# Attention and a maxout layer on one core: weight differences moved up in VectorE's order, half of the copies of transposed w2 on ScalarE, h of the second block ahead of x of the second group

## The chip, the core and the metric

The kernel runs on one core of a Trainium2 chip. A core has TensorE (matmuls; PE in the profile, with its weight loads as PEld), VectorE (DVE), ScalarE (ACT), GpSimd (POOL) and SyncE (SP, which here only issues transfers). Each engine works through its own instructions in program order, and the engines wait for each other with semaphores. The metric is the device time of one launch in microseconds, the median of several runs.

## The reference

Block-causal attention over 8 batches, 8 heads, 576 positions and head size 64 (blocks of 64 positions; a position sees its own block and all earlier ones), and then a maxout layer over the 4608 tokens:

```python
def _attn_ref(q, k, v) -> np.ndarray:
    ...
    scores = scale * np.matmul(q, k.transpose(0, 1, 3, 2))
    ...
    attn = attn / (np.sum(attn, axis=-1, keepdims=True) + 1e-09)
    return np.matmul(attn, v).astype(np.float32)

def _moe_ref(x, w1, w2, w_out) -> np.ndarray:
    h1 = x @ w1
    h2 = x @ w2
    g = np.maximum(h1, h2)
    return (g @ w_out).astype(np.float32)
```

x has 512 columns, w1 and w2 are 512 x 1024, w_out is 1024 x 512. Inputs and the output are fp32.

## The kernel before

**An identity saves a matmul.** max(x w1, x w2) = x w2 + max(x (w1 - w2), 0). So the kernel computes d = w1 - w2 once (`diff_w`, into `d_sb`), g = max(x d, 0) (`h_unit`), the product M = w2 w_out once (`m_unit`, into `m_sb`), and y = x M + g w_out (`y_unit`). For M it needs w2 transposed; `bT_unit` does that on TensorE and copies the result from PSUM into `bT_sb`. There are four weight column blocks j of 256 columns: each has one difference (1024 elements per partition), and one `bT_unit` of eight 128 x 128 transposes and one copy (line 229). h unit f covers 128 columns of d, so h units 2j and 2j+1 read difference j.

**Attention.** Two heads make a pair (32 pairs), two pairs a group (16 groups g). `load_qk` brings q and k of a group, GpSimd casts them to bf16 (`cast`, line 132), TensorE transposes them (`transposes`, line 352), and two engines copy the result from PSUM (line 360). Scores are matmuls into one of two PSUM buffers (`ps_s`), ScalarE takes the exponential (line 395), GpSimd clears the masked corners. `av` multiplies by v (line 479); VectorE takes the reciprocal of the sums (line 485) and multiplies (line 486) into `xp`. `x_out` transposes xp of a group on TensorE (lines 517 and 519) and copies it into `xT` (lines 522 and 523), the x of the maxout layer. All other PSUM results share one pool of four buffers (`ps_m`, tag "m"), handed out in turn.

**Order.** The order is written out by hand: each call below appends to the queues of the engines that it uses. The maxout units stand in a list, `todo`, in a fixed order: for the first 256 tokens h 0, h 1, bT 0, h 2, h 3, bT 1 and so on, then h of the next 320 tokens, then the M units, then y. Each has a number of matmuls, a cost for each (256 columns cost 0.5, 320 cost 0.625, a transpose of w2 0.25) and the number of tokens of x that it needs. `fill(n)` emits units from the list until a cost of n is used up; it takes the first whose tokens are done (`done_tokens`). `fill_of(g)` spreads the ready work over the groups to come.

**The stretch that the change touches** is lines 641 to 682, batch 0's last attention work and the start of batch 1. GpSimd's part of it: five loads of v of batch 1 (lines 651 and 652), and `load_qk(3, ..., gated=True)` at line 653. "Gated" means that GpSimd first writes one column of the destination (line 119), so that the transfer, issued by SyncE, can't start before GpSimd gets there. Later (lines 671 to 680) GpSimd casts q and k of group 3, and TensorE transposes them in the middle of a `fill` of n:

```python
    cast("q", 3, ((pool, 0, RPP),))
    cast("k", 3, ((pool, 0, RPP),))
    n = fill_of(GPB)
    fill(n // 2)
    transposes("q", 3, (dve, act))()
```

By the code's counts n is 32 here: 16 before the transposes of q, about 26 matmuls of 320 columns.

Of the kernel before, what the change touches and what calls it, by code (L numbers as in the profile page):

```python
# [14 lines left out]
def kernel(  # L15
# [10 lines left out]
    nc = tc.nc  # L26
# [83 lines left out]
    dve, pool, act = nc.vector.tensor_copy, nc.gpsimd.tensor_copy, nc.scalar.copy  # L110

    def load_qk(g, queues, gated=False):
        b, u = divmod(g, GPB)
        for nm, src, queue in (("q", q, queues[0]), ("k", k, queues[1])):
            if queue is None:
                continue
            raws[nm, g] = t = raw.tile([P, 2, RPP * D], FP32, name=f"{nm}raw")
            if gated:
                nc.gpsimd.memset(t[:, 0, :1], 0.0)
            queue.dma_start(  # L120
                out=t[:],
                in_=src[b, 4 * u:4 * u + 4].rearrange(
                    "(s h) (p t) d -> (h p) s (t d)", h=2, t=RPP),
            )

    def cast(nm, g, parts):
        t = raws[nm, g].rearrange("p s (t d) -> p t s d", d=D)
        if (nm, g) not in qk_n:
            qk_n[nm, g] = qkn.tile([P, RPP, 2, D], BF16, name=f"{nm}n")
        n = qk_n[nm, g]  # L130
        for copy, j0, j1 in parts:
            copy(out=n[:, j0:j1], in_=t[:, j0:j1])  # L132
# [27 lines left out]
    def diff_w(j):  # L160
        fs = slice(j * WB, (j + 1) * WB)
        nc.vector.tensor_sub(d_sb[:, :, fs], w1_raw[j][:], w2_sb[j])  # L162
# [8 lines left out]
    dve, pool, act = nc.vector.tensor_copy, nc.gpsimd.tensor_copy, nc.scalar.copy  # L171
# [51 lines left out]
    def bT_unit(j):  # L223
        pt = ps_m.tile([P, 2, NDM, P], BF16, name="ps_bT", tag="m")
        for i in range(2):
            for c in range(NDM):
                nc.tensor.transpose(pt[:, i, c, :], w2_sb[j][:, c, i * P:(i + 1) * P], ident[:])
                if i == 1 and c == NDM - 1:
                    nc.vector.tensor_copy(
                        out=bT_sb[:, 2 * j:2 * j + 2, :],  # L230
                        in_=pt.rearrange("p i c d -> p i (c d)"))
                yield
# [52 lines left out]
    def plan():  # L285
        def h(i, f):
            t0, w = spans[i]
            units.append((h_unit(i, f), t0 + w, w / SPAN, NDM))

        def y(i, s, last=False):  # L290
            t0, w = spans[i]
            if last:
                units.append((y_last(i, s), t0 + w, 0.333, 3 * NY))
            else:
                units.append((y_unit(i, s), t0 + w, 1.0, NY))

        for i in range(NSPAN):
            for f in range(NFF):
                h(i, f)
                if i == 0 and f % 2:  # L300
                    units.append((bT_unit(f // 2), 0, 0.25, 2 * NDM))
                if i > 2 and f % 2 == 0 and f // 2 < tiles[i - 1]:
                    y(i - 1, f // 2)
            if i == 1:
                for n in range(2 * NDM):
                    units.append((m_unit(n // NDM, n % NDM), 0, 0.5, NFF))
                for j in range(2):
                    for s in range(tiles[j]):
                        y(j, s)
        n = tiles[-1]  # L310
        for s in range(n):
            y(NSPAN - 1, s, s == n - 1)
# [9 lines left out]
    def fill(n):  # L322
        while n > 0:
            if not current:
                k = next((k for k, t in enumerate(todo) if t[2] <= done_tokens[0]), None)
                if k is None:
                    return max(0, n)
                current.append(todo.pop(k))
            t = current[0]
            next(t[1])  # L330
            n -= t[3]
            t[0] -= 1
            if not t[0]:
                current.pop()
        return 0
# [96 lines left out]
    def tile_0(p):  # L432
        u = ps_s.tile([P, 2, 512], FP32, name="ps_s", tag="s")
        scores(p, u, 0, 0, 0, 512)
        return lambda: (exp(p, u, 512, 0), mask(p, 0))

    def tile_1(p):
        u = ps_s.tile([P, 2, 512], FP32, name="ps_s", tag="s")
        scores(p, u, 0, 0, 512, 64)
        scores(p, u, 64, 1, 128, 448)  # L440
        return lambda: (exp(p, u, 512, 512), mask(p, 576))

    def tile_2(p):
        u = ps_s.tile([P, 2, 512], FP32, name="ps_s", tag="s")
        corner_scores(p, u, 320)
        scores(p, u, 0, 2, 256, 320)
        scores(p, u, 384, 3, 448, P)

        def out():
            exp(p, u, 512, 1024)  # L450
            nc.scalar.activation(
                out=aT_r[p % NA][BLK:, :, 1536:AW], in_=u[BLK:, :, 320:320 + BLK],
                func=AF.Exp, scale=scale,
            )
            mask(p, 1024)
            mask(p, 1344)
        return out

    def region(*tiles):
        for out in tiles:  # L460
            out()

    def av(p, ts):
        b, hp = divmod(p, HP)
        vv = vv_r[b % NV]
        a = aT_r[p % NA]
        n = len(ts)
        h0 = hp // 2 * 4 + hp % 2
        if p % 2 == 0 and ts[0] == 0:
            xps[p // 2] = xpool.tile([P, 2, NCH, 2, D], BF16, name="xp")  # L470
        xp = xps[p // 2]
        po = ps_m.tile([P, n, 2, D + 1], FP32, name="ps_o", tag="m")
        n_mm = 2 * sum(t + 1 for t in ts)
        mm = 0
        for gi, t in enumerate(ts):
            for hh in range(2):
                for c in range(t + 1):
                    a0 = a_col(p, c, t)
                    nc.tensor.matmul(  # L479
                        po[:, gi, hh, :], a[:, hh, a0:a0 + P], vv[:, c, h0 + 2 * hh, :],  # L480
                        start=(mm == 0), stop=(mm == n_mm - 1),
                    )
                    mm += 1
        rec = small.tile([P, 3, 2, 1], FP32, name="rec")
        nc.vector.reciprocal(rec[:, :n, :, 0], po[:, :, :, D])  # L485
        nc.vector.tensor_mul(  # L486
            xp[:, :, ts[0]:ts[0] + n, p % 2].rearrange("q s t d -> q t s d"), po[:, :, :, :D],
            rec[:, :n].to_broadcast([P, n, 2, D]),
        )

    def x_by_dma(g):
        return BY_DMA <= g < NG - 1
# [10 lines left out]
    def x_out(g, t0=0, t1=NCH, copies=(dve, dve)):  # L503
        b, u = divmod(g, GPB)
        if x_by_dma(g):
            if u == GPB - 1:
                done_tokens[0] = (b + 1) * S
            return
        xp = xps[g]
        n = t1 - t0  # L510
        n_odd = min(t1, NCH - 1) - t0
        pe = ps_m.tile([P, 2, n, BLK], BF16, name="ps_xe", tag="m")
        po = ps_m.tile([P, 2, n_odd, BLK], BF16, name="ps_xo", tag="m")
        for s in range(2):
            for t in range(t0, t1):
                src = xp[:, s, t].rearrange("p a d -> p (a d)")
                nc.tensor.transpose(pe[:, s, t - t0, :], src[:BLK], ident[:BLK, :BLK])
                if t < NCH - 1:
                    nc.tensor.transpose(po[:, s, t - t0, :], src[BLK:], ident[BLK:, BLK:])
        dst = xT[:, 2 * u:2 * u + 2, b * S + t0 * P:b * S + t1 * P].rearrange(  # L520
            "p s (t h w) -> p s t h w", h=2, w=BLK)
        copies[0](out=dst[:, :, :, 0], in_=pe[:])
        copies[1](out=dst[:, :, :n_odd, 1], in_=po[:])
        if u == GPB - 1:
            done_tokens[0] = min(b * S + t1 * P, (b + 1) * S)
# [126 lines left out]
        load_v(1, c)  # L652
    load_qk(3, (SP, SP), gated=True)
    x_out(0, 2, NCH)
    fill(2)
    diff_w(1)
    outs = tile_0(4), tile_1(4)
    av(3, [2, 3, 4])
    region(*outs)
    x_out(1, 2, NCH)  # L660
    fill(4)
    diff_w(2)
    fill(2)
    region(tile_2(4), tile_0(5))
    fill(4)
    diff_w(3)
    fill(2)
    region(tile_1(5), tile_2(5))
    fill(4)
    fill(2)  # L670
    cast("q", 3, ((pool, 0, RPP),))
    cast("k", 3, ((pool, 0, RPP),))
    n = fill_of(GPB)
# [86 lines left out]
```

The softmax here doesn't subtract the row's maximum and nothing guards it: scores larger than these inputs give would overflow.

## Time and profile before

| what | before |
|---|---|
| device time, median of 3 runs | 260.99 us (260.82 to 261.92) |
| span of the profiled execution | 259.2 us |
| PE busy | 244.8 us, 94% |
| DVE busy | 137.6 us, 53% |
| ACT busy | 141.3 us, 55% |
| POOL busy | 109.8 us, 42% |
| granted TensorE clock | 1.0 |
| PE's share of the chain that ended last | 85% |
| one weight difference on DVE (line 162) | 1.22 us, four of them |
| one copy of transposed w2 on DVE (line 229) | 0.69 us, four of them |

A busy share is an average over the whole span; TensorE at 94% still has stretches in which it stands. The profile cuts the span into 40 slices of 6.48 us and gives the busy share of each engine in tenths, which shows where those stretches are. For each of them the trace then tells which instruction waited, for which engine and line, and for how long. The chain that ended last is followed back from the last instruction, at each step to what released it; a stretch of the span in which the chain lies on another engine, or on a transfer, isn't set by TensorE.

### The profile page before, as it was taken

How to read it: one execution, taken by the hardware profiler on the slowest of the kernel's cores; microseconds unless marked ns; L12 is line 12 of the kernel's file. 1: busy time of each engine (PE TensorE's matmuls, PEld its weight loads, DVE VectorE, ACT ScalarE, POOL GpSimd, SP SyncE). 2: the span in 40 equal slices, each digit the busy share in tenths (PEclk: the TensorE clock that was granted, in tenths of full speed). 3: DMA queues.
4: the chain of work that ended last, by engine and by line, in shares of the span. 5: the costliest groups of instructions: out<-in, count | busy, mean ns of one | idle time of the engine just before them, and what ended most of it. 6: DMA issues, size and time to landing. Idle time of an engine off the chain costs nothing.

```text
span 259.2 us, 7161 instructions
## 1 busy us (share of the span) xinstructions
PE 244.8 (94%) x2949; PEld 139.4 (54%) x2983; DVE 137.6 (53%) x301; ACT 141.3 (55%) x198; POOL 109.8 (42%) x274
## 2 busy tenths in 40 slices
PE   8688799999999999999999999999999999999995
PEld 3346566856555545454646464646464655444444
DVE  4967996646584518451855185518550853453200
ACT  2798552766665766576657665776577431100111
POOL 2987914475638163816381638263823010000000
DMA  7999998789579995998599949984986122202122
GB/s 245 317 204 310 194 241 146 280 73 275 111 184 250 135 195 136 238 149 215 129 236 139 179 163 239 141 208 139 90 106 116 44 51 83 83 0 81 43 104 99
DMA packets 71265, 41.30 MB, mean 159 GB/s; under 512 B 53568, under 2 KB 58048, under 8 KB 71232
## 3 DMA queue, kind: packets, MB, share of 16 engines
q1 hardware_dynamic: 28544, 31.27, 41.4%
q0 software_dynamic: 42272, 8.92, 38.2%
q10 hardware_dynamic: 416, 0.66, 0.7%
q8 instruction: 23, 0.38, 0.6%
q14 instruction: 10, 0.08, 0.1%
HBM read 34.60 MB, written 9.44 MB: 170 GB/s over the span
## 4 chain that ended last, share of the span: by engine, by line
PE 85%; DMA 5%; POOL 3%; issue 2%; ACT 2%; DVE 1%; POOLq 0%; ACTq 0%
PE ps_y L257 35%; PE ps_h L215 22%; PE ps_o L479 10%; PE ps_s L371 8%; DMA qraw<-in_q_dram 5%; PE ps_M L238 3%; PE ps_qT L352 2%; PE ps_kT L352 2%; POOL vv L136 1%; ACT aT L395 1%; PE ps_y L272 1%; DVE qn L132 1%; PE ps_w L341 1%; PE ps_s L389 1%; POOL wo_sb L168 1%
## 5 line engine op out<-in xcount | busy, mean ns | idle before, releaser
L395 ACT ACTIVATE aT<-ps_s 128x1024 bf16<-128x1024 f32 (+2 forms) x100 | 95.9, 996 | 28.6 <-PE ps_s L371 26.6
L215 PE MATMUL ps_h<-xT,d_sb 128*128 128x512 bf16 (+3 forms) x306 | 67.4, 357 | 2.7 <-DVE d_sb L162 1.2
L257 PE MATMUL ps_y<-wo_sb,g 128*128 128x512 bf16 x275 | 69.1, 379 | 0.4 <-issue 0.3
L220 DVE TENSOR_SCALAR g<-ps_h 128x512 bf16<-128x512 f32 (+3 forms) x80 | 50.8, 636 | 30.2 <-PE ps_h L215 28.4
L400 POOL MEMSET aT<- 64x128 bf16 x124 | 22.4, 199 | 85.1 <-ACT aT L395 84.4
L485 DVE RECIPROCAL rec<-ps_o 128x4 f32<-128x4 f32 (+1 forms) x64 | 12.0, 188 | 62.7 <-PE ps_o L479 61.9
L215 PEld LDWEIGHTS <-d_sb 128*128 128x128 bf16 x320 | 29.1, 98 | 30.1 <-issue 2.7
L479 PEld LDWEIGHTS <-aT 128*128 128x128 bf16 x960 | 37.2, 98 | 13.5 <-issue 0.8
L262 ACT COPY y<-ps_y 128x512 f32<-128x512 f32 x31 | 18.2, 587 | 44.8 <-PE ps_y L257 32.6
L257 PEld LDWEIGHTS <-g 128*128 128x128 bf16 x280 | 25.9, 98 | 29.7 <-issue 1.9
L479 PE MATMUL ps_o<-vv,aT 128*128 128x65 bf16 x960 | 39.8, 194 | 0.0
L257 PE MATMUL ps_y<-m_sb,xT 128*128 128x512 bf16 x128 | 36.5, 380 | 1.2 <-issue 0.8
L136 POOL DMA_DIRECT2D vv<-in_v_dram x40 | 33.6, 847 | 1.6 <-issue 1.2
L371 PE MATMUL ps_s<-qT,kT 64*128 64x64 bf16 (+6 forms) x344 | 31.0, 280 | 1.9 <-ACT kT L360 0.7
L486 DVE TENSOR_TENSOR xp<-ps_o,rec 128x256 bf16<-128x256 f32 (+1 forms) x64 | 31.4, 491 | 2.2
L360 ACT COPY qT<-ps_qT 128x576 bf16<-128x576 bf16 (+1 forms) x17 | 10.3, 614 | 20.0 <-PE ps_qT L352 20.0
L132 POOL CAST qn<-qraw 128x1152 bf16<-128x1152 f32 (+1 forms) x16 | 17.0, 1061 | 8.7 <-DMA qraw<-in_q_dram 8.7
L257 PEld LDWEIGHTS <-xT 128*128 128x128 bf16 x140 | 12.2, 98 | 15.1 <-issue 3.5
L371 PEld LDWEIGHTS <-kT 64*128 64x128 bf16 x344 | 12.2, 94 | 11.0 <-issue 6.2
L132 POOL CAST kn<-kraw 128x1152 bf16<-128x1152 f32 (+1 forms) x15 | 17.1, 1141 | 1.4 <-DMA kraw<-in_k_dram 1.3
L360 ACT COPY kT<-ps_kT 128x576 bf16<-128x576 bf16 x15 | 9.6, 639 | 14.6 <-PE ps_kT L352 14.6
L207 POOL COPY g<-g 128x512 bf16<-128x512 bf16 x8 | 4.9, 613 | 20.7 <-DVE g L220 20.3
(57 smaller groups left out, 160.8 us busy)
## 6 DMA issues: line engine op xcount, KB each, us to landing
qraw<-in_q_dram SPq DMA_DIRECT2D x16, 576.0 KB, 4.1
out_dram<-y SPq DMA_DIRECT2D x35, 256.0 KB, 3.2
kraw<-in_k_dram SPq DMA_DIRECT2D x15, 576.0 KB, 5.4
vv<-in_v_dram POOLq DMA_DIRECT2D x32, 128.0 KB, 5.2
w1raw<-in_moe_w_dram POOLq DMA_DIRECT2D x4, 512.0 KB, 8.7
xT<-in_moe_w_dram POOLq DMA_DIRECT2D x4, 256.0 KB, 9.1
wo_sb<-in_moe_w_out_dram POOLq DMA_DIRECT2D x2, 512.0 KB, 9.0
kraw<-in_k_dram ACTq DMA_DIRECT2D x1, 576.0 KB, 5.5
```

The lines of the kernel that those rows point to most:

```text
L132: copy(out=n[:, j0:j1], in_=t[:, j0:j1])
L136: nc.gpsimd.dma_start(out=vv_r[b % NV][P - rows:, c, :, :D], in_=v[b, :, c * P:c * P + rows, :].rearrange("h p d -> p h d"),)
L215: nc.tensor.matmul(pt[:, :w], d_sb[:, c, f * P:(f + 1) * P], xT[:, c, t0:t0 + w], start=(c == 0), stop=(c == NDM - 1),)
L220: nc.vector.tensor_scalar_max(g[:, f, m:m + w], pt[:, :w], 0.0)
L257: nc.tensor.matmul(py[:], lhs, rhs, start=(n == 0), stop=(n == len(terms) - 1),)
L262: (dve if i < 2 else act)(out=y[:], in_=py[:])
L360: (copy or copies[i])(out=t[:, p0 * RPP:p1 * RPP].rearrange("q (p j) -> q p j", j=RPP), in_=pts[i][:, :, p0:p1].rearrange("q j p -> q p j"),)
L371: nc.tensor.matmul(ps[:, hh, col:col + w], kT[r, k0:k0 + P], qT[r, q0:q0 + w], start=True, stop=True,)
L395: nc.scalar.activation(out=aT_r[p % NA][:, :, a0:a0 + w], in_=ps[:, :, :w], func=AF.Exp, scale=scale,)
L400: (eng or nc.gpsimd).memset(aT_r[p % NA][BLK:, :, a0:a0 + BLK], 0.0)
L479: nc.tensor.matmul(po[:, gi, hh, :], a[:, hh, a0:a0 + P], vv[:, c, h0 + 2 * hh, :], start=(mm == 0), stop=(mm == n_mm - 1),)
L486: nc.vector.tensor_mul(xp[:, :, ts[0]:ts[0] + n, p % 2].rearrange("q s t d -> q t s d"), po[:, :, :, :D], rec[:, :n].to_broadcast([P, n, 2 ...
```

## The change

It does three things, all between the end of batch 0's attention and the first transposes of group 3.

- The weight differences 1, 2 and 3 are called earlier, so that they stand earlier in VectorE's queue: difference 1 ahead of the first copy of transposed w2, difference 2 between the maxima of h unit 2 and h unit 3, difference 3 ahead of the scores' fill instead of in its middle. The h units that read them are meant to find them done.
- The copies of transposed w2 of blocks 1 and 3 go to ScalarE, those of blocks 0 and 2 stay on VectorE. VectorE gets two copies fewer.
- h units 2 and 3 of the first 256 tokens (the second weight block) and the transposes of w2 of block 1 come ahead of `x_out(1, 2, NCH)`, the x of the second group, where TensorE waits for VectorE's `xp`.

```diff
@@ -226,7 +226,7 @@
                 if i == 1 and c == NDM - 1:
-                    nc.vector.tensor_copy(
+                    (act if j % 2 else dve)(
                         out=bT_sb[:, 2 * j:2 * j + 2, :],
                         in_=pt.rearrange("p i c d -> p i (c d)"))
@@ -652,22 +652,20 @@
     x_out(0, 2, NCH)
+    diff_w(1)
     fill(2)
-    diff_w(1)
     outs = tile_0(4), tile_1(4)
     av(3, [2, 3, 4])
     region(*outs)
+    fill(2)
+    diff_w(2)
+    fill(4)
     x_out(1, 2, NCH)
-    fill(4)
-    diff_w(2)
-    fill(2)
     region(tile_2(4), tile_0(5))
-    fill(4)
     diff_w(3)
-    fill(2)
+    fill(6)
     region(tile_1(5), tile_2(5))
-    fill(4)
-    fill(2)
+    fill(6)
```

## The prediction

> **What bounds the kernel now.** I read the page's first two parts first. TensorE is busy 244.8 us of 259.2 (94%), VectorE and ScalarE are near 54%, and in the 40 slices PE shows 9 nearly everywhere except slices 4 to 6 (25.9 to 38.9 us), where it shows 7, 7 and 8. The change edits exactly that stretch. So the question is what TensorE waits for there, and I asked for its waits between 18 and 52 us; the columns are total us, times, longest.
>
> ```profile
> PE ps_xe L517 <- DVE xp L486: 1.2, 1, 1.2
> PE ps_h L215 <- DVE d_sb L162: 1.2, 2, 0.6
> PE ps_qT L352 <- POOL qn L132: 0.6, 1, 0.6
> ```
>
> Three waits: the x transposes of group 1 wait for VectorE's normalisation of pair 3; two h units wait for weight differences; and the q transposes of group 3 wait for GpSimd's cast of q. VectorE's timeline over the same stretch (start, length, what) shows why the first exists.
>
> ```profile
> 26.31 0.69 DVE L229 COPY bT_sb<-ps_bT 128x1024 bf16<-128x1024 bf16 x1
> 26.92 1.24 DVE L162 TENSOR_TENSOR d_sb<-w1raw,xT 128x1024 bf16<-128x1024 f32 x1
> 28.08 0.18 DVE L485 RECIPROCAL rec<-ps_o 128x6 f32<-128x6 f32 x1
> 28.29 0.56 DVE L486 TENSOR_TENSOR xp<-ps_o,rec 128x384 bf16<-128x384 f32 x1
> 30.61 1.22 DVE L162 TENSOR_TENSOR d_sb<-w1raw,xT 128x1024 bf16<-128x1024 f32 x1
> 33.31 1.22 DVE L162 TENSOR_TENSOR d_sb<-w1raw,xT 128x1024 bf16<-128x1024 f32 x1
> ```
>
> TensorE's own timeline gives the restarts and, in the last bracket, the third wait.
>
> ```profile
> 26.74 0.91 PE L479 MATMUL ps_o<-vv,aT 128*128 128x65 bf16 x24
> 31.89 1.05 PE L215 MATMUL ps_h<-xT,d_sb 128*128 128x256 bf16 x8 [0.63 <-DVE d_sb L162]
> 34.59 1.05 PE L215 MATMUL ps_h<-xT,d_sb 128*128 128x256 bf16 x8 [0.60 <-DVE d_sb L162]
> 35.92 3.69 PE L215 MATMUL ps_h<-xT,d_sb 128*128 128x320 bf16 x26
> 40.23 0.43 PE L352 MATMUL ps_qT<-ident,qn 64*128 64x64 bf16 x18 [0.62 <-POOL qn L132]
> ```
>
> The last view decides: the chain that ended last, in order of time.
>
> ```profile
> 29.61 1.59 POOL vv L136 x2
> 31.20 0.11 POOL qraw L119
> 31.31 0.03 POOL kraw L119
> 31.34 7.57 DMA qraw<-in_q_dram
> ...
> 39.03 1.15 POOL qn L132
> 40.18 0.05 issue
> 40.23 0.43 PE ps_qT L352 x18
> ```
>
> From 27 to 40.23 us the chain isn't on TensorE or VectorE. It is five v loads issued by GpSimd, a one-column memset that gates q of group 3, the q transfer, and its cast. TensorE reaches the transposes of that q at 39.61 and stands 0.62 us. What the change saves ahead of that point only makes that wait longer, unless the load moves too.
>
> [...]pair 3's matmuls end at 27.65, yet its reciprocal starts at 28.08, after the copy and the difference queued ahead. [...]after the 1.25 us gap before 28.91 the granted clock still reads 1.00. [...]Here the trace shows no cost: two GpSimd weight-load issues from 17.08 on take 0.76 and 0.75 us beside the first difference (17.23 to 18.45), and two at 14.05 take 0.77 and 0.76 without one.
>
> **The change part by part.**
>
> *Differences earlier.* Number and length stay: four of 1.22 us. Difference 1 moves ahead of the first transposed-w2 copy. VectorE's copies for x end at 26.17, so difference 1 runs 26.1 to 27.3, the copy (0.69) to 27.95, reciprocal and product (0.74) to 28.65. Before, the product ended at 28.85; only 0.2 us earlier, since the same two operations still stand ahead of it.
>
> *h ahead of x.* This fills the 1.25 us gap. h unit 2 (four 256-column matmuls; eight take 0.89 from 29.18 to the next start at 30.07, so 0.45) needs difference 1, done at 27.3, so it starts at about 27.65; h unit 3 ends at 28.5, transposes of w2 (0.54) at 29.05. The x transposes (0.27) then wait for two of the four rotating PSUM buffers: one from the product (28.65), one from h unit 2, whose maximum (0.43) ends at 29.05. They end at 29.4; the scores of pairs 4 and 5 (0.6) at 30.0. Difference tracking is by region, else h at 29.18 could not have run before the x copies of 29.29 into the same xT; so h unit 3 doesn't wait for difference 2.
>
> *Difference 2 now stands in front of h unit 3's maximum:* VectorE runs maximum 2 to 29.05, difference 2 to 30.2, maximum 3 to 30.55. Queued behind it are the x copies of group 1 (to 31.1), then difference 3 (to 32.25) and two maxima (to 33.0). h unit 4 needs the PSUM buffer of unit 3's maximum: it starts at 30.6, so a wait of 0.6 us remains. h 4, h 5 and w2 transposes end at 32.0. The next scores wait for ScalarE (below) and end at 33.1; h 6 needs difference 3 (32.25), already there: the old 0.60 us wait is gone. h 6, h 7 and transposes (0.89 + 0.54) end at 34.5. Then the 26 matmuls of 3.69 us: TensorE reaches the q transposes at **38.2 instead of 39.61, 1.4 us earlier**.
>
> *Two copies on ScalarE.* VectorE loses 2 x 0.69 = 1.4 us. The trace has no ScalarE copy of 128x1024 from PSUM. The low bound is VectorE's own 0.69; the high one the exp of that shape, 1.02[...]. The 576-column copy takes 0.64 and the 256-column one 0.37, which extrapolates to 1.02; I take 1.02. Copy 1 runs 29.2 to 30.25; ScalarE's exps of pair 4 ended at 28.66 and the next scores end at 30.0, so exps slip by 0.3 us, which costs the second scores a buffer wait of about 0.35 us (in the sum above; 0 at the low bound). Copy 3 follows the exps, ends near 36; ScalarE idles from 36.04 to 40.73 now, and the M units that read it start at 41.4. It costs nothing: that idle time hides it.
>
> *What doesn't move.* The fills after the edit hand out the same 20 costed matmuls as before, so the fill counts and the work from there on are the same. GpSimd's queue up to the gate of q waits only for work before 26.1 us, all untouched. q lands at 38.91, its cast ends at 40.18.
>
> **Sum:** 1.4 us saved before the q transposes, the wait there grows from 0.62 to 2.0 us, net 0. Forecast **261.0 us**, the time of before.
>
> **The rivals.** *A, swallowed (above):* 261.0. For it: the chain view and the 0.62 us wait that already stands. Against: one profiled execution shows one landing time; the seven q loads of the first 60 us took 3.7 to 8.6 us from issue to landing, median 5.1, so this one is slow and may vary. *B, it comes through:* if q lands at least 0.9 us earlier in the changed kernel (less traffic beside it, or a typical run unlike this one), TensorE is the bound here and the whole 1.4 us shows: 259.6. Against: no transfer is moved, and this profiled execution took 260.99, the median itself. Partial savings lie between. *C, contention:* difference 2 now lies at 29.0 to 30.2, over the last v-load issues (29.61 on); were GpSimd held for a whole 1.22 us, gate, q, cast and transposes slip as much: 262.2. Against it are the two undisturbed issues at 17 us. *D, the clock:* a 2.0 us stand at 38.2, close to the 0.6 us one before, might drop the clock[...]. Against it: [...]the 1.25 us stand cost no clock.
>
> **How the numbers follow.** A 0.66; B 0.22, of which 0.17 is nearly whole (beyond 0.5%, that is under 259.7) and 0.05 partial; C 0.05, of which 0.03 passes 262.3; D 0.07. Faster 0.17, same 0.66 + 0.05 + 0.02 = 0.73, slower 0.10. The range runs from B's 259.6 to C's 262.2. It leaves out D, the tail of C and a little below B, under 0.2 together, and covers before's own runs (260.82 to 261.92). The ScalarE bounds only change how long TensorE stands before the q transposes.
>
> **What would show it.** In the changed profile: no wait of the x transposes for the product; a wait of h for VectorE of about 0.6 us near 30; the 320-column h matmuls starting near 34.5; ScalarE rows of bT_sb at about 1.02 us; the wait of the q transposes for GpSimd's cast about 2 us; q landing near 38.9 and those transposes still at about 40.2. It is wrong if the q transposes start 1 us earlier (B), if the gate memset comes later than 31.3 (C), if the clock reads under 1.00 near 40 us (D), or if the times after 40 us differ in any other way, which I have no mechanism for.

## The result and the profile after

The changed kernel takes 264.33 us (median of 4 runs, 263.88 to 264.76) against 260.90 us (260.73 to 261.92): the ratio is **1.0123, 95% interval 1.0091 to 1.0155**, slower by 3.4 us. The forecast was 261.0 with a range of 259.6 to 262.2. The result lies above the range.

The page of the changed kernel has a line that the page of before doesn't have: the TensorE clock that was granted, in tenths, for the 40 slices.

```profile
PEclk9999995999999999999999999999999999999999
```

The 5 is the seventh slice (6.56 us each, so 39.4 to 45.9 us), just where the prediction put the transposes of q of group 3. TensorE's waits between 18 and 52 us, asked as for the kernel before:

```profile
PE ps_qT L352 <- POOL qn L132: 3.2, 1, 3.2
PE ps_s L389 <- ACT aT L395: 0.4, 1, 0.4
PE ps_h L215 <- DVE d_sb L162: 0.3, 1, 0.3
```

The x transposes' wait of 1.2 us is gone, and the differences' 1.2 us has shrunk to 0.3. So the change did what it is for. But the wait for q has grown from 0.62 to 3.2 us, not to the 2.0 us of the sum. (A stand, below, is such a stretch in which TensorE waits and does nothing.) TensorE's timeline shows the work on both sides of it.

```profile
34.00 3.70 PE L215 MATMUL ps_h<-xT,d_sb 128*128 128x320 bf16 x26
40.88 0.66 PE L352 MATMUL ps_qT<-ident,qn 64*128 64x64 bf16 x18 [3.19 <-POOL qn L132]
41.47 1.78 PE L215 MATMUL ps_h<-xT,d_sb 128*128 128x320 bf16 x6
43.05 2.98 PE L238 MATMUL ps_M<-wo_sb,bT_sb 128*128 128x256 bf16 x13
```

Read the first start and the last two lengths. The 26 matmuls start 1.92 us earlier than before (34.00 against 35.92) and take the same time. The q transposes start 0.65 us later (40.88 against 40.23). The next two groups take nearly twice what they took in the kernel before:

```profile
40.60 0.99 PE L215 MATMUL ps_h<-xT,d_sb 128*128 128x320 bf16 x6
41.42 1.58 PE L238 MATMUL ps_M<-wo_sb,bT_sb 128*128 128x256 bf16 x13
```

The busy times of the changed kernel by windows of 2 us say why; after the window, the columns give its length, the busy time of PE, PEld, DVE, ACT and POOL with counts, then the granted clock (1.00 is full speed), and at the end the DMA share and GB/s.

```profile
38.00:40.00 2.00, 0.00 (x0) 0.00 (x0) 0.00 (x0) 0.00 (x0) 0.32 (x1) 0.95 1.11 338
40.00:42.00 2.00, 1.12 (x21) 0.80 (x22) 0.42 (x1) 0.39 (x1) 0.82 (x1) 0.50 0.57 92
42.00:44.00 2.00, 2.00 (x10) 1.30 (x9) 1.23 (x3) 0.25 (x1) 1.05 (x1) 0.50 0.09 6
44.00:46.00 2.00, 2.00 (x12) 1.16 (x12) 0.42 (x1) 0.00 (x0) 0.18 (x3) 0.50 0.29 23
46.00:48.00 2.00, 2.00 (x33) 1.58 (x34) 1.11 (x3) 0.64 (x1) 0.52 (x4) 0.85 1.01 396
```

The clock falls to half at about 39.8, 2.1 us after the last h matmul ends (37.70). It stays there for 0.2 us of the first window (0.05 x 2 / 0.5), three whole ones and 0.6 us of the last: 6.8 us.

That q comes later was the other surprise. GpSimd's timeline and the chain that ended last:

```profile
26.53 1.14 POOL L378 COPY kz<-kT 128x128 bf16<-128x128 bf16 x2
27.61 4.19 POOL L136 DMA_DIRECT2D vv<-in_v_dram  x5
31.74 0.16 POOL L119 MEMSET qraw<- 128x1 f32 x1
```

```profile
31.93 7.63 DMA qraw<-in_q_dram
...
39.68 1.15 POOL qn L132
```

The transfer takes as long as before (7.63 against 7.57 us), but the gate comes 0.58 us later (31.74 against 31.16), and with it everything behind it. The delay starts at the two copies into kz (keys that the scores of line 389 read), which `pad_keys` puts on GpSimd: 1.14 us, where before the same row read:

```profile
26.55 0.53 POOL L378 COPY kz<-kT 128x128 bf16<-128x128 bf16 x2
```

VectorE's timeline of the changed kernel shows what runs beside it: difference 1, which now starts 0.86 us earlier.

```profile
26.06 1.22 DVE L162 TENSOR_TENSOR d_sb<-w1raw,xT 128x1024 bf16<-128x1024 f32 x1
```

### The profile page after: what moved, and what is told of

It reads as the page before. It is cut to its first block, busy times and chain, and to the rows that moved or that the text cites. A ratio compares the mean times of both kernels' runs of the same rounds, so it can differ in the third digit from the quotient of the medians.

```text
span 262.4 us, 7161 instructions
## 1 busy us (share of the span) xinstructions
PE 247.2 (94%) x2949; PEld 140.6 (54%) x2983; DVE 136.0 (52%) x299; ACT 143.1 (55%) x200; POOL 110.2 (42%) x274
## 4 chain that ended last, share of the span: by engine, by line
PE 87%; POOL 3%; DMA 3%; issue 2%; ACT 2%; DVE 1%; POOLq 0%; ACTq 0%
PE ps_y L257 35%; PE ps_h L215 22%; PE ps_o L479 10%; PE ps_s L371 8%; PE ps_M L238 3%; PE ps_w L341 3%; DMA qraw<-in_q_dram 3%; PE ps_qT L352 2%; PE ps_kT L352 2%; POOL vv L136 1%; ACT aT L395 1%; PE ps_y L272 1%; PE ps_s L389 1%; POOL wo_sb L168 1%; PE ps_xe L517 1%
## 5 line engine op out<-in xcount | busy, mean ns | idle before, releaser
L215 PE MATMUL ps_h<-xT,d_sb 128*128 128x512 bf16 (+3 forms) x306 | 68.2, 361 | 1.8 <-issue 0.9
L479 PE MATMUL ps_o<-vv,aT 128*128 128x65 bf16 x960 | 39.8, 194 | 0.0
L360 DVE COPY qT<-ps_qT 128x576 bf16<-128x576 bf16 (+1 forms) x17 | 12.1, 711 | 3.9 <-PE ps_qT L352 3.8
```

Of the source, the lines that this page charges most:

```text
L215: nc.tensor.matmul(pt[:, :w], d_sb[:, c, f * P:(f + 1) * P], xT[:, c, t0:t0 + w], start=(c == 0), stop=(c == NDM - 1),)
L360: (copy or copies[i])(out=t[:, p0 * RPP:p1 * RPP].rearrange("q (p j) -> q p j", j=RPP), in_=pts[i][:, :, p0:p1].rearrange("q j p -> q p j"),)
L479: nc.tensor.matmul(po[:, gi, hh, :], a[:, hh, a0:a0 + P], vv[:, c, h0 + 2 * hh, :], start=(mm == 0), stop=(mm == n_mm - 1),)
```

## The experiments

**The theory.** Difference 1 runs over GpSimd's copy into kz and holds it up; q is gated and lands later; TensorE, which arrives earlier, stands 3.2 us; its clock halves; the work after the stand runs at half speed. **The rivals:** the new order or the ScalarE copies cost by themselves and the half clock is a by-product; or the slow kz copy was chance.

### The clock, in the changed kernel

```diff
     fill(n // 2)
+    warm_up(10)
     transposes("q", 3, (dve, act))()
```

> The changed kernel with ten 512-column matmuls on zeros, whose result nobody reads, put on TensorE between fill(n // 2) and the transposes of q of group 3, where it stands 3.2 us. Theory 1 (the stand lets the TensorE clock fall to half; the half clock costs about 2.6 us and the later q about 0.65 us): the ten take about 2.2 us of the stand, the clock stays at 1.00, the transposes of q still start near 40.9, and the time falls to about 261.6 us. Theory 2 (the time goes to the new order itself, and the half clock falls on work that waits anyway): about 264 us as before, or more for the added matmuls.

Measured: 261.84 us, 1.0029 of before (1.0019 to 1.0038). Its windows:

```profile
40.00:42.00 2.00, 0.54 (x20) 0.39 (x20) 0.00 (x0) 0.00 (x0) 1.28 (x2) 1.00 0.55 137
42.00:44.00 2.00, 2.00 (x19) 1.65 (x19) 1.72 (x4) 0.64 (x1) 1.09 (x3) 1.00 0.07 4
```

The clock stays at 1.00, although q still comes late (its transposes start at 41.56 in this profile). From 1.0123 to 1.0029 is 0.0094 of 261 us: **the half clock costs 2.5 us**, give or take 0.9 by the two intervals. Adding useless work to the changed kernel makes it faster, which the rival can't explain.

### Difference 1 put back

```diff
-    diff_w(1)
     fill(2)
+    diff_w(1)
     outs = tile_0(4), tile_1(4)
```

> The changed kernel with difference 1 put back behind the first copy of transposed w2 in VectorE's order; TensorE's order is untouched. Theory 1a (difference 1 holds up GpSimd's copy into kz, which holds up the gate of q): the slow kz copy goes from 0.9 us back to 0.3, the gate and the landing of q move back by 0.6 us (q at about 38.9, transposes at about 40.2), TensorE stands about 2 us instead of 3.2 before them. If 2 us is too short to lower the clock: about 261 us. If it is not: about 263.5 us. Theory 2 (the kz copy was slow by chance): the gate stays near 31.8 and the time near 264.

Measured: 260.83 us, 0.9997 (0.9983 to 1.0010). In this kernel's GpSimd timeline the kz copies take half as long and the gate is back:

```profile
26.56 0.53 POOL L378 COPY kz<-kT 128x128 bf16<-128x128 bf16 x2
27.03 4.18 POOL L136 DMA_DIRECT2D vv<-in_v_dram  x5
31.17 0.15 POOL L119 MEMSET qraw<- 128x1 f32 x1
```

TensorE stands 1.4 us before the q transposes in the profile, and the clock stays at 1.00. One execution in 20 took 263.37 us with a mean clock of 0.993, all others 260.50 to 261.61 with 0.998 or more. That one wasn't profiled, so how long TensorE stood in it isn't known. As a rule, then, this kernel is what the forecast described: the saving is swallowed and nothing is lost.

### Difference 1 alone, in the kernel before

```diff
-    fill(2)
     diff_w(1)
+    fill(2)
     outs = tile_0(4), tile_1(4)
```

> The kernel before with one edit: difference 1 ahead of fill(2), so ahead of the first copy of transposed w2. Theory 1a [...]: one kz copy takes about 0.9 us, the gate comes at about 31.8, q's transposes at about 40.8, TensorE stands about 1.3 us before them, too short for the clock: about 261.6 us, 0.6 over before. Theory 2 (chance): 261.0 us.

Measured: 261.96 us, 1.0036 (1.0024 to 1.0047), with the clock at 1.00. Its GpSimd row:

```profile
26.80 1.15 POOL L378 COPY kz<-kT 128x128 bf16<-128x128 bf16 x2
```

This one moved instruction costs 0.9 us and doubles the kz row. TensorE stands 2.0 us here, more than the 1.3 us expected, because q is also slower to come in this profile: from its gate to its cast it takes 8.35 us (32.03 to 40.38) against 7.87 before (31.16 to 39.03):

```profile
41.58 0.44 PE L352 MATMUL ps_qT<-ident,qn 64*128 64x64 bf16 x18 [1.98 <-POOL qn L132]
```

So a stand of 1.98 us, as long as the 2.0 us that the prediction reckoned with, left the clock at 1.00 in this profile, and none of the 19 executions had a mean clock under 0.998.

Over all thirteen kernels of this study the two copies took 1.14 or 1.15 us in the five with difference 1 ahead of the first fill, and 0.53 us in the eight with it behind. That isn't chance. In the kernel with the ten matmuls, which has the order of the change, the two copies can be told apart (least, median and longest in ns, then first and last start):

```profile
L378 POOL COPY kz<-kT x2: 298/604/909, 26.8 to 27.6; 128x128 bf16<-128x128 bf16 x2
```

It is the first one that takes 0.9 us: it starts at 26.77 and ends at 27.68, just after difference 1 (26.31 to 27.52 there). What the runs show is that the order decides how long this copy takes, by 0.6 us; what the two engines contend for, and which property of the subtraction does it, isn't shown. Beside the copy of transposed w2, which stood in this place before (26.31 to 27.00), the kz copies took 0.53 us.

### A late q in the kernel before

```diff
-    load_qk(3, (SP, SP), gated=True)
     ...
     region(tile_2(4), tile_0(5))
+    load_qk(3, (SP, SP), gated=True)
```

> The kernel before with one edit: the gated load of q and k of group 3 later in GpSimd's order, behind the masks that follow tile_2(4) and tile_0(5), so some 2.6 us later (gate at about 33.8). Nothing of the change is in it. Theory 1 (a stand of TensorE of about 3 us halves its clock for some 5.5 us): TensorE stands about 3.2 us before the transposes of q, the clock reads 0.50 after it, and the time is 261.0 + 2.6 + 2.6 = about 266 us. Rival (the half clock comes from something else in the changed order): the clock stays at 1.00 and the time is about 263.6 us, the delay alone.

Measured: 265.42 us, 1.0171 (1.0136 to 1.0206). Nothing of the change is in it, yet its clock halves too:

```profile
42.87 0.44 PE L352 MATMUL ps_qT<-ident,qn 64*128 64x64 bf16 x18 [2.91 <-POOL qn L132]
```

```profile
42.00:44.00 2.00, 1.13 (x24) 0.89 (x25) 0.66 (x1) 0.63 (x1) 1.79 (x2) 1.00 0.02 7
44.00:46.00 2.00, 2.00 (x11) 1.39 (x10) 0.89 (x3) 0.01 (x1) 0.26 (x3) 0.50 0.34 39
46.00:48.00 2.00, 2.00 (x28) 1.31 (x26) 0.77 (x2) 0.31 (x1) 0.00 (x0) 0.65 0.98 381
```

Here the fall comes at about 44.0, over a microsecond after TensorE has started again, and lasts 2 us and 1.4 us of the next window: 3.4, half as long as in the changed kernel. That the clock's term is smaller here than the 2.6 us expected fits this.

The same with the ten matmuls of the first experiment:

> The kernel just described, with ten 512-column matmuls on zeros, whose result nobody reads, ahead of the transposes of q of group 3. Theory 1: the clock stays at 1.00 and only the delay is left, about 263.6 us. Rival: no difference from the kernel without them, whichever time that has.

Measured: 264.25 us, 1.0117 (1.0091 to 1.0143), clock 1.00. The delay alone is 3.1 us, somewhat over the 2.6 us expected (the gate stands at 34.02 us in this profile, 2.9 us later than before); the clock makes up the other 0.0054 of 261, or 1.4 us. The two intervals overlap a little, so this 1.4 us is known only to about 1.1 us either way.

### q early

```diff
+    load_qk(3, (SP, SP), gated=True)
     for c in range(NCH):
         load_v(1, c)
-    load_qk(3, (SP, SP), gated=True)
```

In the changed kernel:

> The changed kernel with the gated load of q and k of group 3 ahead of the five loads of v of batch 1 in GpSimd's order. Theory 1 (late q is what the saved time runs into): q is gated some 4 us earlier, at about 27.6, lands by about 36 and its cast is done before TensorE comes to it at 37.7; no stand, clock 1.00, and the saving of about 1.9 us comes through: about 259 us. Theory 2: [...]q lands no earlier than 38, TensorE still stands, and the time is over 262 us.

Measured: **258.70 us, 0.9901 (0.9875 to 0.9927)**. q's cast starts at 35.93 and TensorE goes from the h matmuls to the transposes without a wait:

```profile
34.54 3.69 PE L215 MATMUL ps_h<-xT,d_sb 128*128 128x320 bf16 x26
38.17 0.44 PE L352 MATMUL ps_qT<-ident,qn 64*128 64x64 bf16 x18
```

In the kernel before:

> The kernel before with one edit: the gated load of q and k of group 3 ahead of the five loads of v of batch 1 in GpSimd's order. Theory 1 (late q is the last wait in this stretch, 0.62 us in before; the rest are VectorE's 2.5 us, which stay): 0.6 us is saved, about 260.4 us. Rival (the early q itself, not the change's new order, made the 258.7 us): about 258.9 us.

Measured: 260.59 us, 0.9981 (0.9971 to 0.9991). Early q alone is worth 0.5 us, and the change alone loses 3.4 us; together they gain 2.6. The order of the change frees time on TensorE, and only with q early does it count.

With difference 1 put back as well:

> The changed kernel with the gated load of q and k of group 3 ahead of the loads of v of batch 1 (258.7 us alone) and difference 1 put back behind the first copy of transposed w2. With q early the held-up kz copy has slack, so its removal saves nothing; what counts is TensorE's arrival at the transposes of q, about 0.5 us later with difference 1 back. Theory 1: about 259.2 us. Rival (the contention costs wherever it lies): about 258.1 us.

Measured: 259.52 us, 0.9952 (0.9936 to 0.9967), 0.8 us worse than without by the medians. So where q has slack, taking away the held-up kz copy gains nothing. That the earlier difference is then of use isn't shown: in the profiles TensorE comes to the transposes of q only 0.2 us later than without (38.38 against 38.17). It then stands 0.7 us for q of the next group, which the other kernel doesn't. The gate of that q came earlier (38.23 against 39.06), but its transposes started 8.97 us after the gate (at 47.20), against 7.28 in the other kernel (at 46.34, without a wait for q); why stays open.

### The other two parts alone, in the kernel before

The copies on ScalarE:

> The kernel before with one part of the change: the copies of transposed w2 of blocks 1 and 3 on ScalarE. Theory 1 (whatever reaches the transposes of q earlier is lost while q comes at 40.2): VectorE loses 0.69 us between differences 2 and 3, the second wait of h for a difference shrinks, TensorE stands about 1.2 us instead of 0.6 before the transposes of q, clock 1.00, time 261.0 us. Rival (the ScalarE copies are what costs): slower than 262 us.

Measured: 260.88 us, 1.0002 (0.9990 to 1.0014). The time is as expected, the way to it isn't: TensorE stands 0.4 us before the transposes of q, not 1.2. By an estimate it comes there at about 39.55, hardly earlier than before (39.61): q's cast ends at 39.91, and the transposes followed it by 0.05 us in the kernel before. One wait for a difference is gone, and a new wait of 0.3 us of the scores for ScalarE stands in the profile.

The h units ahead of x:

```diff
-    x_out(1, 2, NCH)
     fill(4)
     diff_w(2)
     fill(2)
+    x_out(1, 2, NCH)
```

> The kernel before with one part of the change: h units 2 and 3, difference 2 and the transposes of w2 of block 1 ahead of x_out(1, 2, NCH); difference 1 stays behind the first copy of transposed w2. Theory 1: the wait of 1.25 us of the x transposes is filled, TensorE comes to the transposes of q up to 1.2 us earlier and stands up to 1.9 us there, no held-up kz copy, q as before; the clock mostly holds: 261.0 us, with single executions up to 263.5 where it does not. Rival (the new order costs by itself): over 262 us.

Measured: 260.96 us, 0.9984 (0.9969 to 0.9999). The x transposes' wait is gone; TensorE's waits in its profile begin:

```profile
PE ps_h L215 <- DVE d_sb L162: 1.6, 3, 0.6
PE ps_qT L352 <- POOL qn L132: 1.0, 1, 1.0
```

Neither part costs anything by itself. What the second frees goes to a third wait for a difference and to the wait for q.

Last, the changed kernel with q early and all copies back on VectorE:

> The changed kernel with the gated load of q and k of group 3 ahead of the loads of v (258.7 us), and all copies of transposed w2 back on VectorE. With q early, TensorE's arrival counts, so this measures what the ScalarE copies are worth. Theory 1: VectorE gets 0.69 us back in front of difference 3, so h 6 waits somewhat longer, while ScalarE's exps come about 0.6 us earlier, which frees the scores' buffers: about 258.9 us, within 0.3 of the kernel without this edit. Rival (the ScalarE copies are the useful part): about 259.5 us or more.

Measured: 258.66 us, 0.9904 (0.9884 to 0.9925). The ScalarE copies are worth nothing that these runs can tell.

## Why the prediction was wrong

**Right.** The bound: from 27 to 40 us the chain lies on GpSimd's issues and the transfer of q, and time saved on TensorE ahead of the q transposes isn't gained. The h units ahead of x alone (0.9984) and the change with difference 1 put back (0.9997) show it. The work earlier on: TensorE was to arrive at 38.2 and did at 37.70; the x transposes at 29.1, measured 28.87; the ScalarE copy 1.02 us, measured 1.01; a wait for VectorE of 0.6 us near 30, measured 0.3.

**The first failed step** is the sentence "GpSimd's queue up to the gate of q waits only for work before 26.1 us, all untouched". It is true of semaphores and it isn't enough: an instruction can be held up while it runs (here one kz copy, 0.90 us instead of 0.30). The prediction looked for such a cost at two weight-load issues beside the first difference and found none (0.76 and 0.75 us, against 0.77 and 0.76 without it). It then looked for a collision of difference 2 with the v loads (rival C; the five loads took 4.19 us against 4.18) and didn't lay difference 1's new place, 26.1 to 27.3, beside GpSimd's timeline, where the two kz copies stand at 26.55. They are even links of the chain that ended last, just ahead of the part of it that the prediction shows (kernel before):

```profile
26.55 0.53 POOL kz L378 x2
27.08 1.89 POOL vv L136 x3
```

The term was taken as 0; difference 1 moved alone measured 0.9 us.

**The second failed step** is rival D, a chance of 0.07. It rested on the stand of 2.0 us (measured 3.2, since TensorE came 0.5 us earlier than forecast and q 0.65 us later) and on one stand in the trace of the kernel before, 1.25 us at full clock; how long a stand keeps the clock, and what losing it costs, that trace doesn't show. Measured, stands of 3.2 and 2.9 us halved the clock. It fell 2.1 us after the last matmul in the changed kernel and some 4 us after it in the kernel with the late q. The half clock lasted 6.8 us in the changed kernel and cost 2.5 us. The last section has what the traces show of the moment of the fall.

A slip in the reading ahead of the steps: the prediction gave PE's digits for 25.9 to 38.9 us as 7, 7 and 8. The page shows 7 for 25.9 to 32.4 us and 9 for the two slices after it. The steps rest on the waits and timelines, not on these digits.

**The combination.** C and D were weighed as alternatives. They add up, because the late q lengthens the very stand that lowers the clock: 0.9 us and 2.5 us make the 3.4 us. With the forecast of 261.0 that is 264.4. (C had the kind of collision right and the place wrong: difference 1 and the kz copy, not difference 2 and the v loads.)

## What to carry to other kernels

An edit that brings TensorE earlier to a wait that doesn't move can cost time: it lengthens a stand, and stands of about 3 us here cost 1.4 and 2.5 us through the clock, while those of 1.4 and 2.0 us kept full clock in their profiles (that 2.0 us is safe in general isn't shown: see the last section). When an instruction moves, lay its new interval beside the other engines' timelines, not only its waits, and above all beside the links of the chain that ended last. If a chain view shows a late transfer behind the stretch that you tune, move the transfer first: here 258.7 us instead of 264.3.

## What the hardware showed that was not expected

The moment of the fall doesn't go with the stand alone. It came 2.1 us after the last matmul in one kernel and in another 4 us after it, when TensorE had already been working for 1.1 us; the half clock lasted 6.8 us in one profile and 3.4 in the other. The four executions of the changed kernel had mean clocks of 0.986 (three) and 0.992, those of the late q 0.986 to 0.994.

Windows of 0.5 us narrow the moments down. In the changed kernel:

```profile
39.50:40.00 0.50, 0.00 (x0) 0.00 (x0) 0.00 (x0) 0.00 (x0) 0.32 (x1) 0.79 0.93 278
46.50:47.00 0.50, 0.50 (x10) 0.42 (x5) 0.34 (x1) 0.31 (x1) 0.00 (x0) 0.88 1.01 401
```

At half clock for 0.21 us of the first and 0.12 us of the second, the clock falls at 39.79 and is back at 46.62. In the kernel with the late q it reads 1.00 up to 44.0, and its return is in this window, at 47.40:

```profile
47.00:47.50 0.50, 0.50 (x19) 0.45 (x18) 0.00 (x0) 0.00 (x0) 0.00 (x0) 0.60 1.05 410
```

The stands before the transposes of q in the profiles, and the clock with them:

| kernel | stand, us | granted clock |
|---|---|---|
| changed | 3.19 | half, from 2.1 us into the stand, for 6.8 us |
| late q | 2.91 | half, from 1.1 us after the stand, for 3.4 us |
| difference 1 alone | 1.98 | 1.00 |
| changed, ten matmuls | 1.46 | 1.00 |
| changed, difference 1 put back | 1.40 | 1.00 |

None of these stands lies between 1.98 and 2.91 us, and no run moved a stand or varied its length step by step. So what sets the moment of the fall, and why the half clock lasted twice as long in one kernel as in the other, isn't shown.

A GpSimd copy of 0.30 us took 0.9 us beside one VectorE subtraction of 1.22 us, but the same subtraction cost the kz copies nothing where it started at 26.92, after both had begun.
